# Decode attention with a gated MLP on one core: the last two heads' last keys loaded last over 128 partitions, six heads projected ahead of them, 24 heads projected in halves, result rows 4 apart

## The chip, the cores and the metric

One NeuronCore of a Trainium2 chip runs the kernel; the program uses 1 core. The metric is the device time of one execution in microseconds (us), median of the runs. TensorE (PE in the profile, its weight loads PEld), VectorE (DVE), ScalarE (ACT), GpSimd (POOL) and SyncE (SP) each work through a list of their own; DMAs are issued from the lists of SP and ACT.

## The reference: what is computed

One decode step for 8 sequences (B = 8, one new token each, D = 576), 32 heads of 128 elements, 4096 cached keys and values per head, all bf16:

```python
q = (x @ wq) -> [8, 32, 1, 128];  p = softmax(q . k_cache * 128**-0.5)
a = (p @ v_cache) -> [8, 1, 4096] @ wo
b = gelu(layernorm(x) @ w1 + b1) @ w2 + b2          # F = 4608
g = sigmoid((x * gate_w).sum(-1))
out = g * a + (1 - g) * b                            # [8, 1, 576]
```

The two caches hold 8 x 32 x 4096 x 128 x 2 bytes = 268 MB each, and every byte is read once.

## The kernel before

**Tiling.** The work goes through 32 groups n = 0 to 31; group n is 8 heads (head group hg = n // 8) of one sequence b = n % 8. A group's cache slice lies in SBUF as 128 partitions x 256 keys x 128 elements: partition = head x 16 + row, each row with 256 consecutive keys. That is 8192 KB for K and as much for V, with 64 KB in each partition. "Keys" below are these positions t = 0 to 255 of a partition.

**A group.** `scores` (line 488) takes 32 keys at a time: VectorE multiplies K by q (line 465), TensorE sums the products over slices of the 128 elements (lines 476 and 179), VectorE reduces the rest (line 484). `softmax` (line 500) makes E = exp(s - max) on ScalarE and P, which is E masked to each partition's own head, for all 8 heads (line 513). `pv` (line 520) multiplies P with V: four keys at a time, 32 columns of P as the weights and 4 x 128 elements of V as the moving side, in four column groups of the array. `evict` (line 538) copies the sum out of PSUM, `gather` (line 542) adds up the parts with a selection matrix, `total` (line 533) sums the softmax denominators, `norm` (line 549) divides, and `put` (line 455) writes the result into `OT_sb`, 128 elements x (32 heads x 8 sequences).

**Order.** The order on each engine is the order in which the Python code appends operations; `Stream.emit` puts semaphore waits before them. Groups 1 to 30 run in a loop on TensorE and VectorE. All K, V and weight loads are issued by SP, in order: K of group n + 1 when half of K of group n has been read (line 313), V of group n when `pv` of group n - 1 is done (line 324).

**The MLP** runs in group 0: `up_proj`, `act_h` (writes `hT_sb`), `down_proj` (line 601) with `quarters` (line 587), which splits the 576 output columns in four quarters of 144 (QN) and puts each on its own 32 partitions of PSUM bank `y_ps`, in rows 32 i to 32 i + 7. The last part of V of group 0 is issued after `down_proj`. `load_b2`, `b_gate` add the bias and multiply by 1 - g, into `bmg_sb`. `g4` holds g and 1 - g in the rows of `y_ps`.

**The end.** `to_rows` (line 626) rearranges heads 0 to 23 of `OT_sb` during the last group's scores, and `a_proj` (line 642) multiplies them with wo, 96 matmuls through `quarters`, into `y_ps`. V of the last group comes in 8 pieces of 128, 32, 32, 16, 16, 16, 8 and 8 keys (`V_LAST`, line 334). The first three go through `pv`, `evict` and `gather`; the last five (64 keys, `pv_turned`, line 649) with V as the weights and P's 8 columns as the moving side, so that they add to the gathered sum directly. Then follow `norm_turned` (line 660), `a_proj` of heads 24 to 31 (32 matmuls), one VectorE operation (line 735: g times the attention part plus `bmg_sb`), and 4 DMAs that write the result, two from SP and two from ACT.

Of the kernel before, what the change touches and what calls it, by code (L numbers as in the profile page):

```python
# [7 lines left out]
ALU = mybir.AluOpType  # L8
# [28 lines left out]
QP = 96 + B  # L37
# [103 lines left out]
def bass_gated_mix__mha_block_cached__mixer_channel_mlp__decode_kernel(  # L141
# [23 lines left out]
    def pstride(t):  # L165
        return t[tuple([slice(None)] * len(t.shape))].ap[0][0]
# [55 lines left out]
    hT_sb = sb("hT_sb", [128, NJ, B], BF16)  # L222
# [5 lines left out]
    OT_sb = sb("OT_sb", [128, H, B], BF16)  # L228
# [42 lines left out]
    def load(engine, dst, src, name, waits=()):  # L271
        return op(engine, lambda e: e.dma_start(dst, src), waits, dma=(nc.alloc_semaphore(name), 16))  # L272
# [9 lines left out]
    c_g4 = op("gpsimd", lambda e: e.memset(g4[:], 0.0))  # L282
    ld_x = load("scalar", x_sb, x_flat, "ld_x")
# [36 lines left out]
    def load_v(n, t0=0, t1=NTT, waits=()):  # L320
        nV[0] += 1
        src = kv_src(A_v_cache, n)[:, t0:t1, :]
        dst = VB[:, t0:t1, :]
        t = op("sync", lambda e: e.dma_start(dst, src), [*waits, v_done.get(n - 1)], dma=(sV, 16 * nV[0]))
        v_land[n] = [(t, VB, 0, 0, NTT)]

    def load_v_part(n, buf, at, t0, t1, waits):

        src = kv_src(A_v_cache, n)[:, t0:t1, :]
        dst = buf[:, at:at + t1 - t0, :]  # L330
        t = load("sync", dst, src, f"sVp{n}_{t0}", waits)
        v_land.setdefault(n, []).append((t, buf, at - t0, t0, t1))

    V_LAST = (128, 32, 32, 16, 16, 16, 8, 8)
    T_TURN = NTK + 64
# [119 lines left out]
    def put(n):  # L455
        hg, b = divmod(n, B)
        a_O[n] = op("scalar", lambda e: e.activation(  # L457
            out=OT_sb[:, hg * HB:(hg + 1) * HB, b], in_=O_n[:, :], func=ACT.Copy), [v_norm[n]])
# [61 lines left out]
    def pv(n, parts):  # L520
        for i in parts:
            land, buf, shift, t0, t1 = v_land[n][i]
            for tq in range(t0 // TQ, t1 // TQ):
                j, at = tq % 4, tq * TQ + shift
                o = o_ps[n // last][32 * j:32 * j + 32, :]
                w = [land, v_P[n], a_ev.get(n - 1), *c_ps] if tq == t0 // TQ else ()
                p_pv[n] = op("tensor", lambda e, o=o, tq=tq, at=at, buf=buf: e.matmul(  # L527
                    o, lhsT=(P if n < last else P_last)[:, tq, :, :].rearrange("p h t -> p (h t)"),
                    rhs=buf[:, at:at + TQ, :].rearrange("p t d -> p (t d)"),
                    start=(tq < 4), stop=(tq >= (NTQ if n < last else T_TURN // TQ) - 4)), w)  # L530
        v_done[n] = p_pv[n]
# [10 lines left out]
    def gather(n):  # L542
        o = oz_ps[:, 0:HB] if n < last else qb_ps[:, 0:HB]
        for tt in range(TQ):
            p_oz[n] = op("tensor", lambda e, tt=tt: e.matmul(  # L545
                o, lhsT=O_sb[:, tt, :], rhs=selO[:, tt, :], start=(tt == 0 and n < last), stop=(tt == TQ - 1 and n < last)),
                [a_ev[n], v_norm.get(n - 1), c_selO] if tt == 0 else ())
# [22 lines left out]
    def act_h():  # L570
        hb, t2 = (up[:, i, :] for i in range(2))
        b1b = bass.AP(tensor=b1_sb, offset=0, ap=[[pstride(b1_sb), 128], [1, NJ], [0, B]])
        t = op("scalar", lambda e: e.activation(out=hb, in_=up_ps[:, 0:NJ * B], func=ACT.Copy), [st["p_up"]])
        hbv = hb.rearrange("p (f b) -> p f b", b=B)
        t = op("gpsimd", lambda e: e.tensor_tensor(out=hbv, in0=hbv, in1=b1b, op=ALU.add), [t, ld_b1])
        t = op("gpsimd", lambda e: e.tensor_tensor(out=t2, in0=hb, in1=hb, op=ALU.mult), [t])
        t = op("gpsimd", lambda e: e.tensor_scalar(out=t2, in0=t2, scalar1=0.044715, scalar2=1.0, op0=ALU.mult,
                                                   op1=ALU.add), [t])
        t = op("gpsimd", lambda e: e.tensor_tensor(out=t2, in0=t2, in1=hb, op=ALU.mult), [t])
        t = op("scalar", lambda e: e.activation(out=t2, in_=t2, func=ACT.Sigmoid, scale=gelu_c), [t])  # L580
        st["v_h"] = op("gpsimd", lambda e: e.tensor_tensor(
            out=hT_sb[:].rearrange("p f b -> p (f b)"), in0=hb, in1=t2, op=ALU.mult), [t])
# [4 lines left out]
    def quarters(lhsT, w, first, stop, waits, end=aside):  # L587

        for i in range(4):
            last = (end if i == 3 else aside)("tensor", lambda e, i=i: e.matmul(  # L590
                y_ps[32 * i:32 * i + B, 0:QN], lhsT=lhsT, rhs=w[:, i * QN:(i + 1) * QN], start=first, stop=stop),
                waits if i == 0 else ())
        return last

    def load_b2():
        st["ld_b2"] = [
            load("scalar", b2_4[32 * i + r:32 * i + r + m, :],
                 bass.AP(tensor=B_b2.tensor, offset=B_b2.offset + i * QN, ap=[[0, m], [1, QN]]), f"ld_b2{i}_{r}", [c_b2])
            for i in range(4) for r, m in ((0, 5), (5, 3))]

    def down_proj(j0, j1):
        for jt in range(j0, j1):
            st["p_down"] = quarters(hT_sb[:, jt, :], w2_sb[:, jt, :], jt == 0, jt == NJ - 1,
                                    [st["ld_w2"], st["v_h"], c_yps] if jt == 0 else (),
                                    op if jt in (j0, NJ - 1) else aside)
            st.setdefault("p_down0", st["p_down"])
# [5 lines left out]
    def b_gate():  # L612
        t = op("gpsimd", lambda e: e.tensor_tensor(
            out=bmg_sb[0:QP, :], in0=bmg_sb[0:QP, :], in1=b2_4[0:QP, :], op=ALU.add), [st["a_bx"], *st["ld_b2"]])
        st["g_bmg"] = op("gpsimd", lambda e: e.tensor_scalar(
            out=bmg_sb[0:QP, :], in0=bmg_sb[0:QP, :], scalar1=g4[0:QP, 1:2], scalar2=None, op0=ALU.mult), [t, a_g4])

# [8 lines left out]
    def to_rows(hg):  # L626

        o = OT_sb[:, hg * HB:(hg + 1) * HB, :]
        a = bass.AP(tensor=OT_sb, offset=o.offset, ap=[[pstride(OT_sb), 128], [B, HB], [0, RD], [1, B]])
# [3 lines left out]
        for h in range(HB):  # L633
# [5 lines left out]
            out=o.rearrange("p r b -> p (r b)"), in_=up_ps[:, 0:RD * B], func=ACT.Copy), [st["p_rows"]])  # L639
        st["rows", hg] = st["a_rows"]  # L640

    def a_proj(hg):
        for h in range(hg * HB, (hg + 1) * HB):
            st["p_a"] = quarters(OT_sb[:, h, :], wo_sb[:, h, :], h == 0, h == H - 1,
                                 [st.get(("rows", hg)), a_O.get(min(hg * B + B - 1, NG - 2)), v_norm.get(NG - 1),
                                  st["ld_wo" if hg < NHG - 1 else "ld_wo3"], st["a_bx"]] if h == hg * HB else ())


    def pv_turned(n, parts):
        for i in parts:  # L650
            land, buf, shift, t0, t1 = v_land[n][i]
            for t in range(t0, t1):
                p_oz[n] = op("tensor", lambda e, t=t, buf=buf, at=t + shift: e.matmul(  # L653
                    qb_ps[:, 0:HB], lhsT=buf[:, at, :], rhs=P_last[:, t // TQ, :, t % TQ], start=(t == T_TURN), stop=(t == NTT - 1)),
                    [land, v_P[n]] if t == t0 else ())
# [4 lines left out]
    def norm_turned(n):  # L660
        hg, b = divmod(n, B)
        v_norm[n] = op("vector", lambda e: e.tensor_tensor(  # L662
            out=OT_sb[:, hg * HB:(hg + 1) * HB, b], in0=qb_ps[:, 0:HB], in1=rz[:, :], op=ALU.mult),
            [p_oz[n], v_rz[n]])
# [5 lines left out]
    for n in range(NG):  # L670
# [14 lines left out]
        if n == 0:  # L685
# [10 lines left out]
            for i in range(4):  # L696
                a_g4 = aside("scalar", lambda e, i=i: e.activation(out=g4[32 * i:32 * i + B, :], in_=stat[:, G_COL:G_COL + 2],
                                                                func=ACT.Copy), [v_omg, c_g4])
# [7 lines left out]
        if n == last:  # L706
            softmax(n)
            for hg in range(NHG - 1):
                a_proj(hg)
        pv(n - 1, (0,))  # L710
        evict(n - 1)
        gather(n - 1)
# [8 lines left out]
    t0 = 0  # L721
    for nt in V_LAST:
        load_v_part(last, VL, t0, t0, t0 + nt, [k_done[last, 0]])
        t0 += nt
    pv(last, (0,))
    total(last)
    recip(last)
    pv(last, (1, 2))
    evict(last)
    pv_turned(last, (3,))  # L730
    gather(last)
    pv_turned(last, range(4, len(V_LAST)))
    norm_turned(last)
    a_proj(NHG - 1)
    t = op("vector", lambda e: e.scalar_tensor_tensor(  # L735
        out=out_sb[0:QP, :], in0=y_ps[0:QP, 0:QN], scalar=g4[0:QP, 0:1], in1=bmg_sb[0:QP, :],
        op0=ALU.mult, op1=ALU.add), [st["p_a"], st["g_bmg"], a_g4])
    ld_out = [load(("sync", "scalar")[i % 2], out_flat[:, i * QN:(i + 1) * QN], out_sb[32 * i:32 * i + B, :],
                   f"ld_out{i}", [t]) for i in range(4)]
# [43 lines left out]
```

## Time and profile before

| | |
|---|---|
| median of 3 runs | 1298.19 us (1298.13 to 1298.19) |
| the profiled execution's own time | 1298.21 us |
| its span in the profile | 1296.3 us |
| busy: PE, PEld, DVE, ACT, POOL | 739.2, 152.9, 851.1, 68.8, 10.4 us |
| moved by DMA | 557.12 MB, 430 GB/s over the span |
| mean granted TensorE clock | 0.83 |

How to read it: the span runs from the first to the last recorded instruction; the execution's own time is 1.9 us longer. Start times below are microseconds from the start of the span. "L653" is line 653. A line of the chain of waits names a start, a length and what that stretch of the end-determining chain was spent on; a line of the timeline names start, length, engine, line, operation, output <- input and the count. In the windows view the columns are: window, its length, then busy time and number of instructions of PE, PEld, DVE, ACT and POOL, then the granted TensorE clock, the mean busy share of the 16 DMA engines, and GB/s.

### The profile page before, as it was taken

Reading aid. Unit: us, or ns where it says so; the run is one execution under the profiler, and the core shown is the slowest. Engines: PE = TensorE matmul, PEld = TensorE weight load, DVE = VectorE, ACT = ScalarE, POOL = GpSimd, SP = SyncE. Lnnn points to the kernel's source line nnn. Section 1 sums busy time; section 2 is a strip of 40 time slices with the busy share of each in tenths; the row PEclk is TensorE's granted clock in tenths of the full one; section 3 lists DMA queues with packets and bytes.
Section 4 is the critical chain, followed back from the end, with each engine's and each line's share of the span. In section 5 each row is a group of like instructions: output and inputs, shape, how many; then the busy total and the mean of one; then the engine's idle time right before and its main releaser. Section 6 shows DMA issues by size and latency. Waiting matters only on the chain.

```text
span 1296.3 us, 10765 instructions
## 1 busy us (share of the span) xinstructions
PE 739.2 (57%) x5044; PEld 152.9 (12%) x3252; DVE 851.1 (66%) x1075; ACT 68.8 (5%) x163; POOL 10.4 (1%) x23
## 2 busy tenths in 40 slices
PE   3955556555556555556555556645556655546646
PEld 0521111011111001111001111001111001111003
DVE  3646667766668766667766667766667776667771
ACT  3100000000000000000000000000000000000000
POOL 0010000000000000000000000000000000000000
PEclk8877898778888877888887799878789877888886
DMA  9999999999999999999999999999999999999997
GB/s 405 430 440 429 441 425 433 441 427 441 427 431 441 427 441 429 431 441 427 439 431 431 441 425 439 433 431 441 425 437 435 429 443 425 437 433 431 441 417 327
DMA packets 12987, 557.12 MB, mean 430 GB/s; under 512 B 1568, under 2 KB 2608, under 8 KB 3504
## 3 DMA queue, kind: packets, MB, share of 16 engines
q1 hardware_dynamic: 12704, 556.93, 99.5%
q8 instruction: 7, 0.11, 0.0%
q10 hardware_dynamic: 272, 0.04, 0.0%
q14 instruction: 4, 0.03, 0.0%
HBM read 556.96 MB, written 0.01 MB: 430 GB/s over the span
## 4 chain that ended last, share of the span: by engine, by line
DMA 68%; DVE 19%; PE 9%; issue 3%; SPq 0%; DVEq 0%
DMA KR<-in_A_k_cache_dram 67%; DVE p L465 16%; PE psb L179 7%; DVE s_sb L484 2%; DMA KR<-in_A_v_cache_dram 2%; PE psb L476 2%; SPq L272 0%; DVEq L134 0%; PE psb L590 0%; PE psb L653 0%; DVE out_sb L735 0%; DVE OT_sb L662 0%
## 5 line engine op out<-in xcount | busy, mean ns | idle before, releaser
L465 DVE TENSOR_TENSOR p<-KR,q_n 128x4096 bf16<-128x4096 bf16 x256 | 582.0, 2284 | 229.7 <-DMA KR<-in_A_k_cache_dram 229.7
L179 PE MATMUL psb<-p,ident 128*128 128x512 bf16 x1792 | 482.9, 415 | 0.0
L476 PE MATMUL psb<-p,ident 128*128 128x512 bf16 x256 | 111.4, 435 | 504.5 <-DVE p L465 504.5
L484 DVE TENSOR_REDUCE s_sb<-psb 128x32 f32<-128x512 f32 x256 | 175.2, 684 | 90.8 <-PE psb L179 90.8
L476 PEld LDWEIGHTS psb<-p,ident 128*128 128x128 bf16 x256 | 26.1, 102 | 950.9 <-DVE p L465 950.4
L527 PE MATMUL psb<-VB,P 128*32 128x512 bf16 x1984 | 115.0, 385 | 4.5 <-DMA VB<-in_A_v_cache_dram 4.5
L513 DVE TENSOR_SCALAR P<-E,own 128x256 bf16<-128x256 bf16 x248 | 51.7, 284 | 84.3 <-ACT E L510 84.3
L527 PEld LDWEIGHTS psb<-VB,P 128*32 128x32 bf16 x1984 | 50.6, 98 | 54.4 <-DMA VB<-in_A_v_cache_dram 4.7
L452 ACT ACTIVATE q_n<-q_bc 128x128 bf16<-128x128 bf16 x32 | 9.9, 309 | 865.9 <-DVE p L465 865.9
L545 PE MATMUL psb<-selO,O_sb 128*128 128x8 f32 x256 | 33.9, 259 | 21.8 <-ACT O_sb L539 21.8
L545 PEld LDWEIGHTS psb<-selO,O_sb 128*128 128x128 f32 x256 | 31.0, 191 | 37.1 <-ACT O_sb L539 37.1
L539 ACT ACTIVATE O_sb<-psb 128x512 f32<-128x512 f32 x32 | 19.1, 597 | 176.6 <-PE psb L527 176.6
L566 PE MATMUL psb<-yT_sb,KR 128*128 128x8 bf16 (+1 forms) x216 | 19.6, 229 | 0.0
L566 PEld LDWEIGHTS psb<-yT_sb,KR 128*128 128x128 bf16 (+1 forms) x216 | 18.4, 165 | 2.7 <-issue 1.4
L534 PEld LDWEIGHTS psb<-rs,ones 128*128 128x128 f32 x64 | 12.3, 194 | 46.0 <-issue 45.2
L510 ACT ACTIVATE E<-s_sb,mD 128x256 bf16<-128x256 f32 x32 | 16.0, 499 | 9.7 <-DVE mD L509 9.6
L501 DVE TENSOR_REDUCE mA<-s_sb 128x1 f32<-128x256 f32 x32 | 13.4, 420 | 1.1
L516 DVE TENSOR_REDUCE es<-E 128x1 f32<-128x256 bf16 x32 | 13.2, 412 | 0.0
L550 DVE RECIPROCAL rz<-psb 128x8 f32<-128x8 f32 x31 | 6.2, 201 | 9.0 <-PE psb L545 9.0
L457 ACT ACTIVATE OT_sb<-O_n 128x8 bf16<-128x8 bf16 x31 | 7.4, 237 | 84.5 <-DVE O_n L551 84.5
L534 PE MATMUL psb<-rs,ones 128*128 128x8 f32 x64 | 9.4, 219 | 0.0
L517 DVE TENSOR_SCALAR rs<-own,es 128x8 f32<-128x8 f32 x32 | 8.5, 265 | 1.1
(81 smaller groups left out, 109.7 us busy)
## 6 DMA issues: line engine op xcount, KB each, us to landing
KR<-in_A_k_cache_dram SPq DMA_DIRECT2D x2, 4096.0 KB, 27.2
VB<-in_A_v_cache_dram SPq DMA_DIRECT2D x1, 5376.0 KB, 21.0
VB<-in_B_w_dram SPq DMA_DIRECT2D x1, 5184.0 KB, 39.5
KR<-in_B_w_dram SPq DMA_DIRECT2D x1, 4608.0 KB, 43.3
VB<-in_A_wq_dram SPq DMA_DIRECT2D x1, 4096.0 KB, 12.6
KR<-in_A_v_cache_dram SPq DMA_DIRECT2D x1, 4096.0 KB, 17.9
KR<-in_A_wo_dram SPq DMA_DIRECT2D x1, 3456.0 KB, 24.7
VB<-in_A_v_cache_dram SPq DMA_DIRECT2D x1, 2816.0 KB, 38.7
```

The lines of the kernel that those rows point to most:

```text
L179: return e.add_instruction(mybir.InstMatmult(name=nc.get_next_instruction_name(), engine=mybir.EngineType.PE, ins=[e.lower_ap(rhs), e.lowe ...
L465: v_mult[n, c] = op("vector", lambda e: e.tensor_tensor(out=p1[:, par, :, :], in0=k, in1=qb, op=ALU.mult), [k_land[n, s], a_q[n], p_sum.ge ...
L476: fn = lambda e, r=r: e.matmul(tr_ps[par][:, :], lhsT=ident[:, :], rhs=r, start=True, stop=False)
L484: v_red[n, c] = op("vector", lambda e: e.tensor_reduce(out=s_sb[:, at:at + CT], in_=tr_ps[par][:, :].rearrange("p (t c) -> p t c", c=CH), ...
L501: t = op("vector", lambda e: e.tensor_reduce(out=mA[:, 0:1], in_=s_sb[:, :], axis=AX.X, op=ALU.max), [v_red[n, NC - 1], c_mA])
L510: a_exp[n] = op("scalar", lambda e: e.activation(out=E[:, :], in_=s_sb[:, :], func=ACT.Exp, bias=mD[:, 0:1], scale=1.0), [v_nm[n], v_P.get ...
L513: v_P[n] = op("vector", lambda e, h=h: e.tensor_scalar(out=(P if n < NG - 1 else P_last)[:, :, h, :], in0=E[:, :].rearrange("p (q t) -> p ...
L527: p_pv[n] = op("tensor", lambda e, o=o, tq=tq, at=at, buf=buf: e.matmul(o, lhsT=(P if n < last else P_last)[:, tq, :, :].rearrange("p h t ...
L534: p_z[n] = op("tensor", lambda e: e.matmul(oz_ps[:, HB:2 * HB], lhsT=ones[:, :], rhs=rs[:, :], start=True, stop=True), [v_rs[n], v_norm.ge ...
L539: a_ev[n] = op("scalar", lambda e: e.activation(out=O_sb[:].rearrange("p t d -> p (t d)"), in_=o_ps[n // last][:, :], func=ACT.Copy), [p_p ...
L545: p_oz[n] = op("tensor", lambda e, tt=tt: e.matmul(o, lhsT=O_sb[:, tt, :], rhs=selO[:, tt, :], start=(tt == 0 and n < last), stop=(tt == T ...
L566: st["p_up"] = (op if end else aside)("tensor", lambda e, w=w, o=o, kt=kt: e.matmul(o, lhsT=w, rhs=yT_sb[:, kt, :], start=(kt == 0), stop= ...
```

## The change

1. **V of the last group** comes in 10 pieces. Keys 0 to 159 of all heads: 64, 64, 32 (128 partitions, through `pv`). Keys 160 to 255 of the first six heads ("A": 96 partitions): 32, 32, 16, 16. Keys 160 to 255 of the last two heads ("B"): their 32 rows of 96 keys are laid out as 128 partitions x 24 keys, into the space of `q_bc`, in pieces of 8, 8, 8.
2. **Weights for B.** Their probabilities must lie on the same 128 partitions. `exp_wide` (ScalarE) makes exp again in f32 for them, `spread_P` (VectorE, 3 operations) normalizes them, and two small DMAs from SP copy them into `PW` (64 partitions x 24 elements each). `total` and `recip` move ahead of `pv` for this.
3. **The end.** After the A pieces `norm_turned` writes six heads and `norm_first` the partial sums of two; heads 24 to 27 are projected between the first B piece and the second; `norm_wide` finishes the last two heads; heads 28 and 29 are projected in the meantime, 30 and 31 last.
4. **24 heads in halves.** `a_proj_ahead` multiplies heads 0 to 23 with wo in 48 matmuls of 288 columns into bank `up_ps`, four ScalarE copies bring them to `A_f`, and GpSimd multiplies by g and adds them to `bmg_sb`.
5. **Result rows 4 apart.** `quarters` takes 32 weight columns with a stride through `hT_sb` or `OT_sb` (now sequence-major), so that sequence b lands on row 32 i + 4 b, with other sums on the rows between. `g4` is filled by 4 DMAs from ACT, `b2_4` by one DMA instead of 8, and the result is written by one DMA from SP instead of 4.
6. **`keep_busy`** puts 4, 1 and 3 matmuls of 512 columns, whose results nobody reads, between the pieces.

```diff
+    T_ALL = 160
+    HA = HB - 2
+    KW = (NTT - T_ALL) // 4
+    V_LAST = (("all", 64), ("all", 64), ("all", 32), ("A", 32), ("A", 32), ("A", 16), ("A", 16), ("B", 8), ("B", 8), ("B", 8))
+    def load_v_last(n, waits):
...
+            if kind == "B":
+                d = VW[:, t0:t1, :].rearrange("p t d -> p (t d)")
+                s = A_v_cache[b, hg * HB + HA]
+                s = bass.AP(tensor=s.tensor, offset=s.offset + (T_ALL + t0) * DH,
+                            ap=[[NTT * DH, 2 * RH], [KW * DH, 4], [1, nt * DH]])
+            else:
+                rows = 128 if kind == "all" else HA * RH
+                d, s = VL[0:rows, t0:t1, :], src[0:rows, t0:t1, :]
+            v_part.append((kind, t0, t1, load("sync", d, s, f"sVp{i}", waits)))
...
-    def quarters(lhsT, w, first, stop, waits, end=aside):
+    def quarters(t, n, j, w, first, stop, waits, end=aside):
+        lhsT = bass.AP(tensor=t, offset=j, ap=[[pstride(t), 128], [n // BS, 32]])
         for i in range(4):
             last = (end if i == 3 else aside)("tensor", lambda e, i=i: e.matmul(
-                y_ps[32 * i:32 * i + B, 0:QN], lhsT=lhsT, rhs=w[:, i * QN:(i + 1) * QN], start=first, stop=stop),
+                y_ps[32 * i:32 * i + 32, 0:QN], lhsT=lhsT, rhs=w[:, i * QN:(i + 1) * QN], start=first, stop=stop),
                 waits if i == 0 else ())
...
+    def a_proj_ahead():
+        h1 = H - HB
+        for h in range(h1):
+            lhsT = bass.AP(tensor=OT_sb, offset=h, ap=[[pstride(OT_sb), 128], [H // BS, 32]])
+            for i in range(2):
+                t = aside("tensor", lambda e, h=h, i=i, lhsT=lhsT: e.matmul(
+                    up_ps[64 * i:64 * i + 32, 0:2 * QN], lhsT=lhsT, rhs=wo_sb[:, h, 2 * i * QN:2 * (i + 1) * QN],
+                    start=(h == 0), stop=(h == h1 - 1)), [st["rows", NHG - 2], st["ld_wo"]] if h == i == 0 else ())
...
+    def spread_P(n):
+        h = HA * RH
+        t = op("vector", lambda e: e.tensor_tensor(out=rs[h:, :], in0=own[h:, :], in1=rz[h:, :], op=ALU.mult), [v_rz[n]])
+        t = op("vector", lambda e: e.tensor_reduce(out=rz_p[h:, :], in_=rs[h:, :], axis=AX.X, op=ALU.add), [t])
+        t = op("vector", lambda e: e.tensor_scalar(
+            out=P_n[h:, :, 0:KW], in0=E_f[h:, :, 0:KW], scalar1=rz_p[h:, 0:1], scalar2=None, op0=ALU.mult), [t, st["a_Ef"]])
...
+            s = bass.AP(tensor=p1, offset=(h + RH * i) * p + P_n.offset, ap=[[p, RH], [32, 4], [1, KW]])
+            d = bass.AP(tensor=PW, offset=64 * i * q + 32 * i, ap=[[q, 64], [1, KW]])
+            st["ld_PW"].append(load("sync", d, s, f"ld_PW{i}", [t, c_PW]))
...
+    def keep_busy(n):
+        for i in range(n):
+            r = wo_sb[:, i, 0:512]
+            if i == 0:
+                fn = lambda e, r=r: e.matmul(tr_ps[1][:, :], lhsT=ident[:, :], rhs=r, start=True, stop=(n == 1))
+            else:
+                fn = lambda e, r=r, i=i: held(e, tr_ps[1][:, :], ident[:, :], r, i == n - 1)
+            aside("tensor", fn, [v_red[last, NC - 1], st["ld_wo"]] if i == 0 else ())
...
+            p_oz[n] = op("tensor", lambda e, o=o, v=v, p=p, t=t, stop=(end and t == t1 - 1): e.matmul(
+                o, lhsT=v, rhs=p, start=(kind == "B" and t == 0), stop=stop),
+                [land, w, *(st["ld_PW"] if w is None else ())] if t == t0 else ())
...
-    pv(last, (0,))
+    load_v_last(last, [k_done[last, 0], a_q[last]])
     total(last)
     recip(last)
-    pv(last, (1, 2))
+    spread_P(last)
+    pv(last, v_part[0][3], *v_part[0][1:3])
+    keep_busy(4)
+    pv(last, v_part[1][3], *v_part[1][1:3])
+    keep_busy(1)
+    pv(last, v_part[2][3], *v_part[2][1:3])
     evict(last)
-    pv_turned(last, (3,))
-    gather(last)
-    pv_turned(last, range(4, len(V_LAST)))
-    norm_turned(last)
-    a_proj(NHG - 1)
+    keep_busy(3)
+    gather(last, qb_ps[:, 0:HB], False)
+    for i in range(3, 7):
+        pv_turned(last, i)
+    v_A = norm_turned(last)
+    norm_first(last)
+    pv_turned(last, 7)
+    a_proj(H - HB, H - HB + 4, [v_A])
+    pv_turned(last, 8)
+    pv_turned(last, 9)
+    v_B = norm_wide(last)
+    a_proj(H - HB + 4, H - 2, [v_A])
+    a_proj(H - 2, H, [v_B])
...
-    ld_out = [load(("sync", "scalar")[i % 2], out_flat[:, i * QN:(i + 1) * QN], out_sb[32 * i:32 * i + B, :],
-                   f"ld_out{i}", [t]) for i in range(4)]
+    ld_out = [load("sync", by_quarters(out_flat, D), batch_rows(out_sb, QN), "ld_out", [t])]
```

More of the change, by code (lines that the diff above doesn't have):

```diff
@@ L221, in bass_gated_mix__mha_block_cached__mixer_channel_mlp__decode_kernel @@
     b2_4 = sb("b2_4", [128, QN], BF16)
-    hT_sb = sb("hT_sb", [128, NJ, B], BF16)
+    hT_sb = sb("hT_sb", [128, B * NJ + NJ], BF16)
+    hT_b = view(hT_sb, 0, [128, B, NJ])
     Q4 = sb("Q4", [128, 4 * NJ * B], BF16)
@@ L227, in bass_gated_mix__mha_block_cached__mixer_channel_mlp__decode_kernel @@
     q_bc = sb("q_bc", [128, B, NHG * DH], BF16)
-    OT_sb = sb("OT_sb", [128, H, B], BF16)
+    OT_sb = sb("OT_sb", [128, B * H + H], BF16)
+    OT_b = view(OT_sb, 0, [128, B, H])
+    VW = view(q_bc, 0, [128, (B * NHG), DH])
+    PW = sb("PW", [128, 2, 32], BF16)
+    X2 = sb("X2", [128, 2], F32)
+    E_f = view(p1.bitcast(F32), CT * DH // 2 + 2 * QN, [128, 4, 32])
+    P_n = view(p1, CT * DH + 6 * QN, [128, 4, 32])
+    rz_p = sb("rz_p", [128, 1], F32)
+    A_f = view(p1.bitcast(F32), CT * DH // 2, [128, QN])
     bmg_sb = view(up_f, 0, [128, QN])
@@ L457, in put @@
         a_O[n] = op("scalar", lambda e: e.activation(
-            out=OT_sb[:, hg * HB:(hg + 1) * HB, b], in_=O_n[:, :], func=ACT.Copy), [v_norm[n]])
+            out=OT_b[:, b, hg * HB:(hg + 1) * HB], in_=O_n[:, :], func=ACT.Copy), [v_norm[n], c_OT])
     def mult(n, c):
@@ L518, in softmax, with pv @@
             out=rs[:, :], in0=own[:, :], scalar1=es[:, 0:1], scalar2=None, op0=ALU.mult), [t, p_z.get(n - 1)])
[L520 to L530, printed above, removed]
+    def pv(n, land, t0, t1):
+        for tq in range(t0 // TQ, t1 // TQ):
+            j, at = tq % 4, tq * TQ
+            o, v = o_ps[n // last][32 * j:32 * j + 32, :], VB if n < last else VL
+            w = [land, v_P[n], a_ev.get(n - 1), *c_ps] if tq == t0 // TQ else ()
+            p_pv[n] = op("tensor", lambda e, o=o, tq=tq, at=at, v=v: e.matmul(
+                o, lhsT=(P if n < last else P_last)[:, tq, :, :].rearrange("p h t -> p (h t)"),
+                rhs=v[:, at:at + TQ, :].rearrange("p t d -> p (t d)"),
+                start=(tq < 4), stop=(tq >= (NTT if n < last else T_ALL) // TQ - 4)), w)
         v_done[n] = p_pv[n]
@@ L540, in evict, with gather @@
                                                       func=ACT.Copy), [p_pv[n], p_oz.get(n - 1)])
-    def gather(n):
-        o = oz_ps[:, 0:HB] if n < last else qb_ps[:, 0:HB]
+    def gather(n, o, stop=True):
         for tt in range(TQ):
             p_oz[n] = op("tensor", lambda e, tt=tt: e.matmul(
-                o, lhsT=O_sb[:, tt, :], rhs=selO[:, tt, :], start=(tt == 0 and n < last), stop=(tt == TQ - 1 and n < last)),
+                o, lhsT=O_sb[:, tt, :], rhs=selO[:, tt, :], start=(tt == 0), stop=(tt == TQ - 1 and stop)),
                 [a_ev[n], v_norm.get(n - 1), c_selO] if tt == 0 else ())
@@ L638, in to_rows @@
         st["a_rows"] = aside("scalar", lambda e: e.activation(
-            out=o.rearrange("p r b -> p (r b)"), in_=up_ps[:, 0:RD * B], func=ACT.Copy), [st["p_rows"]])
+            out=o.rearrange("p b r -> p r b"), in_=up_ps[:, 0:RD * B].rearrange("p (r b) -> p r b", b=B),
+            func=ACT.Copy), [st["p_rows"]])
         st["rows", hg] = st["a_rows"]
[L642 to L646, printed above, removed]
@@ L649, in pv_turned @@
[L649 to L655, printed above, removed]
+    def a_proj_ahead():
[6 more added lines that the diff above has]
+                    start=(h == 0), stop=(h == h1 - 1)), [st["rows", NHG - 2], st["ld_wo"]] if h == i == 0 else ())
+        for i in range(4):
+            t = aside("scalar", lambda e, i=i: e.activation(
+                out=A_f[32 * i:32 * i + 32, :], in_=up_ps[64 * (i // 2):64 * (i // 2) + 32, i % 2 * QN:(i % 2 + 1) * QN],
+                func=ACT.Copy), [t] if i == 0 else ())
+        t = op("gpsimd", lambda e: e.tensor_scalar(
+            out=A_f[0:QP, :], in0=A_f[0:QP, :], scalar1=g4[0:QP, 0:1], scalar2=None, op0=ALU.mult), [t, *st["a_g4"]])
+        st["g_bmg"] = op("gpsimd", lambda e: e.tensor_tensor(
+            out=bmg_sb[0:QP, :], in0=bmg_sb[0:QP, :], in1=A_f[0:QP, :], op=ALU.add), [t, st["g_bmg"]])
@@ new lines, in a_proj, with exp_wide @@
+    def a_proj(h0, h1, normed):
+        for h in range(h0, h1):
+            st["p_a"] = quarters(OT_sb, H, h, wo_sb[:, h, :], h == H - HB, h == H - 1,
+                                 [a_O[NG - 2], *normed, st["ld_wo3"], st["a_bx"]] if h == h0 else ())
+    def exp_wide(n):
+        h = HA * RH
+        st["a_Ef"] = op("scalar", lambda e: e.activation(
+            out=E_f[h:, :, 0:KW], in_=s_sb[h:, T_ALL:].rearrange("p (s k) -> p s k", s=4), func=ACT.Exp,
+            bias=mD[h:, 0:1], scale=1.0), [v_nm[n]])
@@ L695, in bass_gated_mix__mha_block_cached__mixer_channel_mlp__decode_kernel @@
                                                            scalar1=-1.0, scalar2=1.0, op0=ALU.mult, op1=ALU.add), [a_g])
-            for i in range(4):
-                a_g4 = aside("scalar", lambda e, i=i: e.activation(out=g4[32 * i:32 * i + B, :], in_=stat[:, G_COL:G_COL + 2],
-                                                                func=ACT.Copy), [v_omg, c_g4])
+            st["a_g4"] = a_g4 = [load("scalar", batch_rows(g4, 2, i), stat[:, G_COL:G_COL + 2], f"ld_g4{i}", [v_omg, c_g4])
+                    for i in range(4)]
             down_proj(0, NJ)
@@ L707, in bass_gated_mix__mha_block_cached__mixer_channel_mlp__decode_kernel @@
             softmax(n)
-            for hg in range(NHG - 1):
-                a_proj(hg)
-        pv(n - 1, (0,))
+            exp_wide(n)
+            a_proj_ahead()
+        pv(n - 1, v_land[n - 1], 0, NTT)
         evict(n - 1)
-        gather(n - 1)
+        gather(n - 1, oz_ps[:, 0:HB])
         if n < last:
```

72 lines of the change are left out of this document (46 added, 26 removed).

## The prediction, made before the changed kernel ran

> **What bounds the kernel now.** First the page: the DMA queues, the rates by slice, and the chain that ended last.
>
> ```profile
> GB/s 405 430 440 429 441 425 433 441 427 441 427 431 441 427 441 429 431 441 427 439 431 431 441 425 439 433 431 441 425 437 435 429 443 425 437 433 431 441 417 327
> ...
> q1 hardware_dynamic: 12704, 556.93, 99.5%
> ...
> DMA 68%; DVE 19%; PE 9%; issue 3%; SPq 0%; DVEq 0%
> ```
>
> SP's queue keeps the 16 DMA engines busy for 99.5% of the span, and no slice between the first and the last stands out. The bytes are the same after the change, so nothing can be won or lost ahead of the last slice unless the queue runs dry. What is left is the end; the chain of waits, in order of time, shows it:
>
> ```profile
> 1267.23 24.38 DMA KR<-in_A_v_cache_dram
> 1291.61 0.05 issue
> 1291.66 0.39 PE psb L653 x8
> 1292.05 0.02 issue
> 1292.07 0.20 DVE OT_sb L662
> 1292.28 0.04 issue
> 1292.32 1.16 PE psb L590 x32
> 1293.48 0.03 issue
> 1293.51 0.37 DVE out_sb L735
> ```
>
> The last 8 keys of V land at 1291.61. Their 8 matmuls, the norm and 32 projections take 1.90 us to the final VectorE operation at 1293.51; the output fills the rest to 1296.3. So the whole stake is 4.7 us (0.36%), and a change that only shortens this end can't reach 0.2% (2.6 us, about what a measurement of this kernel can tell from no change). The timeline of TensorE and its neighbours there:
>
> ```profile
> 1243.47 2.84 PE L179 MATMUL psb<-p,ident 128*128 128x512 bf16 x7
> ...
> 1263.75 3.91 SPq L272 DMA_DIRECT2D KR<-in_A_v_cache_dram  x8
> ...
> 1264.00 1.67 PE L179 MATMUL psb<-p,ident 128*128 128x512 bf16 x7
> ...
> 1265.73 1.67 PE L590 MATMUL psb<-KR,OT_sb 128*8 128x144 bf16 x96
> ...
> 1271.92 5.89 PE L527 MATMUL psb<-VB,P 128*32 128x512 bf16 x64 [4.52 <-DMA VB<-in_A_v_cache_dram]
> ...
> 1278.53 1.06 PE L545 MATMUL psb<-selO,O_sb 128*128 128x8 f32 x8 [0.71 <-ACT O_sb L539]
> ...
> 1279.86 0.17 DVE L551 TENSOR_TENSOR O_n<-psb,rz 128x8 bf16<-128x8 f32 x1
> ...
> 1281.64 3.60 PE L527 MATMUL psb<-KR,p 128*32 128x512 bf16 x32 [2.06 <-DMA KR<-in_A_v_cache_dram]
> ...
> 1285.18 0.60 PE L534 MATMUL psb<-rs,ones 128*128 128x8 f32 x2
> ...
> 1285.81 0.21 DVE L658 RECIPROCAL rz<-psb 128x8 f32<-128x8 f32 x1 [5.78 <-PE psb L534]
> ...
> 1287.35 0.60 ACT L539 ACTIVATE O_sb<-psb 128x512 f32<-128x512 f32 x1 [7.05 <-PE psb L527]
> ...
> 1287.88 0.56 PE L653 MATMUL psb<-p,KR 128*128 128x8 bf16 x16 [0.59 <-DMA KR<-in_A_v_cache_dram]
> ...
> 1290.40 0.99 PE L653 MATMUL psb<-p,KR 128*128 128x8 bf16 x24 [0.67 <-DMA KR<-in_A_v_cache_dram]
> ```
>
> Each of these waits tells a landing: keys to 127 at 1281.6, to 207 at 1287.9, to 239 at 1290.4, to 255 at 1291.6. That is 78 ns per key (80 keys in 6.24 us, 32 in 2.52, 16 in 1.21), 32 KB each. The windows view gives the clock:
>
> ```profile
> 1283.60:1287.00 3.40, 3.40 (x34) 1.09 (x26) 0.21 (x1) 0.00 (x0) 0.00 (x0) 0.53 1.00 402
> 1287.00:1290.40 3.40, 2.14 (x48) 1.76 (x41) 0.00 (x0) 0.60 (x1) 0.00 (x0) 0.97 0.81 318
> 1290.40:1293.80 3.40, 2.47 (x64) 1.90 (x64) 0.49 (x2) 0.00 (x0) 0.00 (x0) 0.50 0.02 7
> ```
>
> TensorE runs its last stretch at half clock: 32 projections in 1.16 us there, 96 in 1.67 earlier.
>
> **Part by part: what is hidden.** `down_proj` loads 32 weight columns for each of its 144 matmuls instead of 8, and the last part of V of group 0 is issued behind it:
>
> ```profile
> 14.70 5.59 PE L428 MATMUL psb<-VB,p 128*8 128x512 bf16 x40 [3.04 <-DMA VB<-in_A_wq_dram]
> ...
> 47.56 30.69 SPq L324 DMA_DIRECT2D VB<-in_A_v_cache_dram  x2
> ...
> 73.40 4.49 PE L590 MATMUL psb<-VB,hT_sb 128*8 128x144 bf16 x144 [4.83 <-POOL hT_sb L581]
> ```
> ```profile
> VB<-in_A_v_cache_dram SPq DMA_DIRECT2D x1, 2816.0 KB, 38.7
> ...
> KR<-in_B_w_dram SPq DMA_DIRECT2D x1, 4608.0 KB, 43.3
> ...
> KR<-in_B_w_dram SPq DMA_DIRECT2D x1, 576.0 KB, 44.2
> ```
>
> The load ahead of it, issued at 47.6, lands 38.7 us later, at 86.3, while `down_proj` ends at 77.9: 8 us of cover by the landing. The matmuls could double (4.5 us) unseen; without cover, each microsecond would count in full. The four `g4` DMAs stand in ACT's list where four copies stood, `load_b2` becomes one issue instead of eight, three memsets join GpSimd's start, where TensorE waits for wq until 14.7 anyway: nothing. `a_proj_ahead` has 48 matmuls of 288 columns for 96 of 144, the same columns but in two column groups instead of four: 1.67 us becomes 3.3, in the 4.52 us that TensorE waits for V of group 30. Its four copies and two GpSimd operations have 20 us until they are needed. Were that cover gone, `pv` of group 30 would start later, and it has slack of its own: the first piece of V of group 31 now lands 64 keys earlier, but nothing behind it ends before the last landing.
>
> **The stream.** SP issues 10 pieces, 8 took 3.91 us, so about 4.9 from 1263.75; the queue holds V of group 30 until 1271.9, so they follow without a gap; their second wait, for the last copy out of `q_bc`, ends in group 30. Two more pieces: 0.05 us, between nothing and 0.2 (16 KB rows became 2 KB rows at no more than 1 ns per key above). The A pieces are the unknown: every large load in the trace spans 128 partitions, these 96. By bytes an A key takes 0.75 x 78 = 58 ns, 5.6 us for 96; by length of row it takes 78, 7.5 us. I take bytes, since 96 rows are six for each of 16 engines as 128 are eight, and the row nearest to it is the 78 ns that did not change with the length of the rows. Landings by that: key 159 at 1284.1, A at 1286.0, 1287.9, 1288.8, 1289.8, B at 1290.4, 1291.0, 1291.66.
>
> **TensorE before B.** `total` goes ahead to 1280.1 (after the norm, 1279.86 + 0.17), 0.60; `pv` of 64 keys 1.8 (half of 3.60); four `keep_busy` at 0.24 to 0.41 (1.67 / 7 and 2.84 / 7), 1.3; 64 keys 1.6; one more 0.3; 32 keys 0.85: 1286.5. Eviction 0.7, with three `keep_busy` beside it, and 1.06 of `gather`: 1288.3. Then 96 keys at 35 ns (0.56 / 16; 41 by 0.99 / 24): 3.4 to 3.9, to 1291.7 or 1292.2. That is right where B becomes ready.
>
> **The added wait.** The first B matmul waits for both PW copies, and behind it on TensorE stand the 16 projections of heads 24 to 27, the other 16 B matmuls and the last 16 projections; VectorE's `norm_wide`, the final operation and SP's output wait for those. `recip` now ends near 1281.0, three VectorE operations near 0.2 follow, and SP issues the copies about 1281.8, long after the V pieces on its queue. That queue serves in order: the 576 KB load, 1.4 us by itself, lands 44.2 us after its issue, behind the 4608 KB load. So the copies move only after the last piece of V. Their price isn't in the trace: nothing at least, one 8-key piece (0.62) at most, which has as many rows; they carry 6 KB, not 256, so I take 0.2. The first B matmul starts at 1291.66 + 0.2 + 0.05 = 1291.91.
>
> **The sum from there.** 24 B matmuls 0.84 to 0.99 (0.56 x 24 / 16; the x24 row), 0.90; 16 projections 0.28 to 0.57 (at 1.67 / 96 and 1.13 / 32; the chain's 1.16 includes its tail), 0.40; `norm_wide` as the norm of before, 0.26 with its gaps, heads 28 and 29 beside it; 8 projections 0.14 to 0.39, 0.30, and a 0.03 gap: final operation at 1293.80, against 1293.51: **+0.29**. I take middles because the fuller TensorE may hold its clock. The output:
>
> ```profile
> L272 SPq DMA_DIRECT2D out_dram<-out_sb x2: 298/333/368, 1293.9 to 1294.3; - x2
> ```
>
> SP's second output issue starts about 0.4 after its first; with one issue the data starts that much earlier, less if 32 rows take longer to issue than 8: **-0.30**, between 0 and -0.4. Sum: 0.29 - 0.30, about nothing. On the profiled execution's own 1298.21 (span 1296.3 and 1.9 around it; the median is 1298.19) that gives **1298.2 us**; with its terms at their ends 1297.5 to 1299.0.
>
> **Rivals.**
>
> *Six rows per engine isn't what an A piece costs* (the other side). The mechanism is the slowest engine or memory side of the 96 partitions: if it carries r rows of 24 KB instead of six, A takes r / 6 x 5.6 us, and all landings behind it shift. With r = 8 (an A key as slow as any other, 78 ns) that is +1.9: 1300.1, still no measurable difference. From r = 9 on (more than 2.6 us) it decides for slower; at r = 12, half the engines' or half the memory's rate, +5.6: 1303.8. For it: the trace has no large load under 128 partitions, so it shows 430 GB/s for one layout only, and DMA is what ends last. Against: rows of 8 KB down to 2 KB ran at the same 76 to 79 ns per key, which looks like engines that each work through equal rows. Chances: 0.20 for about eight, 0.20 for nine or more.
>
> [...]
>
> *The PW copies overtake V* (the change gains): B then waits for V alone, two of its pieces and heads 24 to 27 are done ahead, and after 1291.66 stand 0.05 + 0.39 + 0.26 + 0.30 + 0.03: final operation at 1292.69, -0.82, with the output -1.1: 1297.1. For it: they are issued ten microseconds early. Against: the 44.2 us of the 576 KB load. 0.08.
>
> *TensorE becomes the bound* before B: at half clock throughout, with `keep_busy` (8 x 0.41) in the way instead of beside the eviction, A ends near 1292.9 rather than 1291.7, and the B matmuls wait a further 1.0: 1299.2. For it: the clock stayed at 0.53 while TensorE was busy all of 1283.6 to 1287.0. Against: it then rose to 0.97, and the new stream is fuller. 0.10.
>
> **How the numbers follow.** Forecast 0.42, eight rows 0.20, nine or more 0.20, TensorE 0.10, overtaking 0.08. The range leaves out the nine rows or more: 1296.9 (overtaking, with its ends) to 1300.9 (eight rows with the forecast's upper end); the likeliest case alone 1297.5 to 1299.0. Slower by over 0.2% (above 1300.8): nine rows and a little of the eight, 0.22. Faster (below 1295.6): only if most of the end vanished, 0.01. Within 0.2%: 0.77.
>
> **What would show it.** In the profile after, the last V landing at 1291.7 (six rows) or 1293.5 and later; the idle time before the first A matmuls and what ended it; the wait of TensorE ahead of the first B matmul, released by a DMA into PW just after the last V piece (in order) or by V at 1290.4 (overtaking), or no wait at all (TensorE bound); the granted clock from 1287 on; 1.89 us from the first B matmul to the final operation; one output issue. The prediction is wrong if the DMA queue runs dry in group 0, if the A pieces land late by more than 2 us, or if the copies take longer than a V piece.

## The result, and the profile after

The changed kernel takes **1305.09 us** (median of 6 runs, 1304.28 to 1305.69), the kernel before in the same runs 1298.12: a ratio of 1.0053, 95% interval 1.0042 to 1.0064. It is 7.0 us slower. The prediction, 1298.2 with a range to 1300.9, was wrong; the time lies 1.3 us above its rival of twelve rows (1303.8), to which, with all from nine rows on, it gave 0.20. The profiled execution took 1304.28 us, its span is 1302.5.

One thing ahead of the rest: the text and the diff ahead of the prediction have the two PW copies on SP (`load("sync", ...)`). That is wrong. The changed kernel says `load("scalar", ...)`, so ACT issues them, and the prediction's "added wait" rests on the wrong queue.

The page of the profile after, the lines that stood first before:

```profile
GB/s 403 446 422 435 435 427 441 429 439 429 441 427 443 423 441 429 435 435 427 439 431 439 429 441 427 439 427 441 429 435 435 427 439 431 439 429 439 427 417 251
...
q1 hardware_dynamic: 12868, 556.94, 99.5%
...
DMA 69%; DVE 19%; PE 9%; issue 3%; SPq 0%; DVEq 0%
```

The last slice but one moves 417 GB/s in both; only the last falls, from 327 to 251. TensorE takes up V of group 30 at 1271.62, where it was 1271.92 before. So nothing was lost in group 0 or in the loop. The chain of waits at the end:

```profile
1267.53 29.40 DMA KR<-in_A_v_cache_dram
1296.93 0.05 issue
1296.97 0.61 PE psb L738 x16
1297.58 0.02 issue
1297.60 0.17 DVE OT_sb L747
1297.78 0.04 issue
1297.82 0.71 PE psb L617 x16
1298.53 0.52 PE psb L738 x16
1299.05 0.75 PE psb L617 x13
1299.80 0.03 issue
1299.82 0.37 DVE out_sb L836
```

The chain hangs on the last A piece (keys 240 to 255 of six heads), which lands at 1296.93; the forecast was 1289.8. The B pieces, issued after it, land 29.2 us after their issue, the last at 1298.5, just ahead of its matmuls, so they don't end the chain. TensorE's timeline shows which landings were late:

```profile
1271.62 3.64 PE L554 MATMUL psb<-VB,P 128*32 128x512 bf16 x64 [1.97 <-DMA VB<-in_A_v_cache_dram]
...
1281.41 1.05 PE L554 MATMUL psb<-KR,p 128*32 128x512 bf16 x16 [1.55 <-DMA KR<-in_A_v_cache_dram]
...
1287.05 1.04 PE L554 MATMUL psb<-KR,p 128*32 128x512 bf16 x8 [4.27 <-DMA KR<-in_A_v_cache_dram]
...
1293.66 1.01 PE L738 MATMUL psb<-p,KR 96*128 96x8 bf16 x32 [1.82 <-DMA KR<-in_A_v_cache_dram]
1295.33 0.59 PE L738 MATMUL psb<-p,KR 96*128 96x8 bf16 x16 [0.65 <-DMA KR<-in_A_v_cache_dram]
1296.97 0.59 PE L738 MATMUL psb<-p,KR 96*128 96x8 bf16 x16 [1.05 <-DMA KR<-in_A_v_cache_dram]
1297.42 0.35 PE L738 MATMUL psb<-PW,q_bc 128*128 128x2 bf16 x8
```

Key 127 is on time (1281.4), key 159 comes at 1287.05 instead of 1284.1, and A stays late. TensorE waits each time, so it isn't the bound; for the first B matmul it waits for nothing. The windows view, first of the kernel before, then of the changed one (the last three columns are the granted clock, the DMA engines' busy share and GB/s):

```profile
1284.00:1288.00 4.00, 3.41 (x35) 1.06 (x28) 0.21 (x1) 0.60 (x1) 0.00 (x0) 0.65 1.02 407
```
```profile
1284.00:1288.00 4.00, 0.95 (x8) 0.14 (x8) 0.00 (x0) 0.00 (x0) 0.00 (x0) 0.52 1.00 191
1288.00:1292.00 4.00, 3.84 (x47) 2.91 (x41) 0.00 (x0) 0.60 (x1) 0.00 (x0) 0.50 0.99 228
1292.00:1296.00 4.00, 1.61 (x48) 1.44 (x48) 0.00 (x0) 0.00 (x0) 0.00 (x0) 0.50 0.96 246
```

This is the line to learn to see: the busy share stays at 1.0 and the rate halves. The engines aren't short of work; each packet takes twice as long: in the trace's packet records the median packet of 8 KB that starts in the first of these windows took 314 ns before and 599 ns after. Here the DMA engines' busy share was no measure of what they moved: 1.00 at 191 GB/s, 1.02 at 407 before.

### The profile page after: what moved, and what is told of

It is laid out like the page before. It is cut to its first block, busy times and chain, and to the rows that moved or that the text cites. A ratio compares the mean times of both kernels' runs of the same rounds, so it can differ in the third digit from the quotient of the medians.

```text
span 1302.5 us, 10785 instructions
## 1 busy us (share of the span) xinstructions
PE 741.1 (57%) x5052; PEld 155.7 (12%) x3255; DVE 852.4 (65%) x1080; ACT 69.4 (5%) x164; POOL 16.1 (1%) x28
## 3 DMA queue, kind: packets, MB, share of 16 engines
q1 hardware_dynamic: 12868, 556.94, 99.5%
## 4 chain that ended last, share of the span: by engine, by line
DMA 69%; DVE 19%; PE 9%; issue 3%; SPq 0%; DVEq 0%
DMA KR<-in_A_k_cache_dram 66%; DVE p L494 16%; PE psb L180 7%; DVE s_sb L513 2%; DMA KR<-in_A_v_cache_dram 2%; PE psb L505 1%; SPq L283 0%; DVEq L135 0%; PE psb L617 0%; PE psb L738 0%; DVE out_sb L836 0%; DVE OT_sb L747 0%
```

## The experiments

The theory after this profile: loads that touch 96 partitions run at about half rate because of where those partitions lie. Rivals: it is the B layout, the copies or the new end; it is the split of 96 rows over 16 engines; each partition has a rate of its own; it is the side that is read, since with the partitions the rows of the cache change too.

**Same kernel, A over all 128 partitions.**

```diff
-                rows = 128 if kind == "all" else HA * RH
+                rows = 128
```

> The changed kernel with its A pieces loaded over all 128 partitions (786 KB more to move, 1.8 us at 430 GB/s; the extra rows are not used). If the shape of the A pieces, 96 partitions, is what made V late, moving more is faster: last V near 1293.5, time near 1300.2. If it is the B pieces, the two PW copies or the new end, this stays near 1305 or goes to 1307.

Measured: 1299.24 us (1298.89 to 1300.69), ratio to before 1.001 (1.0 to 1.002). Moving 786 KB more is 5.9 us faster than the changed kernel, and 1.0 better than expected. Windows and chain of this run:

```profile
1284.00:1288.00 4.00, 3.22 (x51) 2.03 (x49) 0.00 (x0) 0.60 (x1) 0.00 (x0) 1.00 1.02 412
```
```profile
1267.81 24.10 DMA KR<-in_A_v_cache_dram
...
1294.92 0.37 DVE out_sb L836
```

At the same busy share the rate is back at 412. So the shape of the A loads is the cause, not B, the copies or the end: those are all still in it.

**The kernel before, with nothing but the shape of its last loads changed.**

```diff
...
-        t = load("sync", dst, src, f"sVp{n}_{t0}", waits)
+        if t0 < 160:
+            t = [load("sync", dst, src, f"sVp{n}_{t0}", waits)]
+        else:
+            t = [load("sync", dst[a:b, :, :], src[a:b, :, :], f"sVp{n}_{t0}_{a}", waits) for a, b in ((0, 96), (96, 128))]
...
```

> The kernel before, nothing of the change but the shape of the last loads: each piece from key 160 on is loaded as partitions 0 to 95 and then 96 to 127, same bytes, same order of work. If the 96-partition loads alone carry the loss: by the loads measured alone 72 keys took 8.2 us on 96 partitions and 3.1 on 32, so 96 keys take up to 15.1 us instead of 7.5, and from half of that on if the two overlap: 1302 to 1306. If the loss needs the rest of the change: 1298.3.

Measured: 1304.36 us (2 runs), ratio 1.0049 (1.0031 to 1.0067). The windows view of this run:

```profile
1284.00:1288.00 4.00, 1.46 (x22) 0.44 (x14) 0.21 (x1) 0.00 (x0) 0.00 (x0) 0.92 0.92 197
1288.00:1292.00 4.00, 0.82 (x8) 0.16 (x8) 0.00 (x0) 0.00 (x0) 0.00 (x0) 0.50 1.02 248
```

So the shape is enough by itself: the old kernel shows the same half rate, and nothing else of the change is in it. (The other 32 partitions are a load of their own here, so this run has 96 and 32 partitions and six loads more.)

**Each A piece in two loads, 0 to 31 and 32 to 95.**

```diff
...
+                if kind == "A":
+                    more = load("sync", VL[0:32, t0:t1, :], src[0:32, t0:t1, :], f"sVq{i}", waits)
+                    d, s = VL[32:96, t0:t1, :], src[32:96, t0:t1, :]
...
```

> The changed kernel, each A piece in two loads: partitions 0 to 31, then 32 to 95; the same bytes on the same partitions. Halves theory (partitions 0 to 63 share one half of the memory's DMA side, 64 to 127 the other, 215 GB/s each): 32 to 95 touches both halves evenly and runs at 430 GB/s, 0 to 31 at 215, together 7.3 us for A where 96 rows cost about 12: time near 1300.2. Uneven-split theory (96 rows do not divide well over 16 engines, 64 and 32 do): 5.6 us, time near 1298.5. Per-partition theory (a partition takes 3.4 GB/s, so the rate goes by the number of partitions): 7.5 + 7.5 us, time near 1308.

Measured: 1302.58 us, ratio 1.0035 (1.0022 to 1.0048): 2.5 us better than 96 in one load, on the same partitions, but 2.4 us above the halves theory's number, 4.1 above the uneven split's and 5.4 below the per-partition theory's. No theory is hit. The halves theory is nearest; its two halves were the author's conjecture, with 215 GB/s as half of the 430 of the whole span, and the next two runs test its principle.

**The loads alone.** One load at a time, no computing; the output is zeros. Each shape is loaded with 24 and with 96 keys, four times in one run.

```diff
...
+    SHAPES = (("from0_128", 0, 128), ("from0_96", 0, 96), ("from16_96", 16, 112), ("from0_64", 0, 64),
+              ("from32_64", 32, 96), ("from0_32", 0, 32), ("from48_32", 48, 80))
...
```

> Loads alone, one at a time, of 24 and of 96 keys (6 and 24 KB rows), no computing and an output of zeros; the difference of the two landings is the time for 72 keys, free of what each load costs anyway. Halves theory: 128 partitions 5.5 us; 64 from partition 0 5.5, 64 from partition 32 2.7; 32 from 0 2.7; 96 from 0 at least 5.5 and up to 8.2 if engines block each other; 96 from 16 at least 4.1 and up to 8.2. Uneven-split theory: 64 partitions 2.7 wherever they start, 32 1.4, both 96 alike above 4.1. Per-partition theory: 5.5 for all seven.

The windows view of the 96-key loads, first to seventh shape in the order above (window, its length, GpSimd, clock, DMA share, GB/s):

```profile
6.00:14.40 8.40, 0.00 (x0) 1.00 0.95 374
20.00:31.20 11.20, 0.00 (x0) 1.00 0.93 211
37.00:47.80 10.80, 0.00 (x0) 1.00 0.89 207
54.30:62.30 8.00, 0.00 (x0) 1.00 0.88 187
68.00:72.60 4.60, 0.00 (x0) 1.00 0.81 315
76.70:80.60 3.90, 0.00 (x0) 1.00 0.80 170
85.10:89.00 3.90, 0.00 (x0) 1.00 0.78 176
```

Row four against row five: 64 partitions, the same bytes, as many rows of the same length, and 187 or 315 GB/s (with most of a load's start and end in it) according to whether they begin at 0 or at 32. That excludes the uneven split and a rate per partition. But 96 from 16, with 48 rows in either half, is as slow as 96 from 0, and 32 from 48 as slow as 32 from 0. Two halves are too coarse.

**More shapes.**

```diff
+    SHAPES = (("a", 0, 112), ("b", 0, 80), ("c", 0, 48), ("d", 64, 128), ("f", 16, 80), ("g", 32, 128), ("h", 32, 96))
```

> Loads alone as before (24 and 96 keys, one at a time), more shapes, in this order: 0 to 111, 0 to 79, 0 to 47, 64 to 127, 16 to 79, 32 to 127, 32 to 95. What is open is why 96 partitions from 16, with 48 rows in each half, were as slow as 96 from 0. [...] If only the two halves counted: 16 to 79 4.1, 32 to 127 5.4, 0 to 47 4.1.

The DMA view, issue to landing; 96 keys first, then 24 keys for the same letters:

```profile
a<-in_A_k_cache_dram SPq DMA_DIRECT2D x4, 2688.0 KB, 12.5
g<-in_A_k_cache_dram SPq DMA_DIRECT2D x4, 2304.0 KB, 12.5
...
f<-in_A_k_cache_dram SPq DMA_DIRECT2D x4, 1536.0 KB, 9.6
h<-in_A_k_cache_dram SPq DMA_DIRECT2D x4, 1536.0 KB, 6.2
c<-in_A_k_cache_dram SPq DMA_DIRECT2D x4, 1152.0 KB, 10.8
a<-in_A_k_cache_dram SPq DMA_DIRECT2D x4, 672.0 KB, 4.2
g<-in_A_k_cache_dram SPq DMA_DIRECT2D x4, 576.0 KB, 3.9
...
f<-in_A_k_cache_dram SPq DMA_DIRECT2D x4, 384.0 KB, 3.9
h<-in_A_k_cache_dram SPq DMA_DIRECT2D x4, 384.0 KB, 3.2
c<-in_A_k_cache_dram SPq DMA_DIRECT2D x4, 288.0 KB, 3.5
```

The difference is the time of 72 keys: 32 to 95 (h) 3.0 us; 16 to 79 (f), as many rows, 5.7, where two halves say 4.1; 0 to 47 (c) 7.3 for fewer rows than h, where they say 4.1 as well; 32 to 127 (g) 8.6, where they say 5.4; 0 to 111 (a) 8.3. Of all shapes tried only 32 to 95 (1.18 MB in 3.0 us, 393 GB/s) and the full 128 (374 GB/s with a load's start and end in it) come near the 430 GB/s of the whole span. The other two shapes took 6.1 (64 to 127) and 7.2 (0 to 79). So two halves fail in f, c and g, by 1.4 to 1.8 times. What sets the rate of each shape, and which rows go to which engine, isn't shown here and stays open.

**The copies behind V, on SP's queue** (with A over 128 partitions).

```diff
-            st["ld_PW"].append(load("scalar", d, s, f"ld_PW{i}", [t, c_PW]))
+            st["ld_PW"].append(load("sync", d, s, f"ld_PW{i}", [t, c_PW]))
```

> The version with A over 128 partitions, and the two PW copies issued by SP behind V instead of by ACT. If SP's queue serves in order, the first B matmul waits for the copies, which land after the last piece of V: the final operation about 1 us later than in that version (1299.24), 1300.2. If copies overtake, no difference: 1299.2.

Measured: 1301.06 us, ratio 1.0024 (1.0014 to 1.0033), 1.8 us above the same kernel with ACT's queue (about 1 was expected). Its timeline:

```profile
1294.18 0.35 PE L738 MATMUL psb<-PW,q_bc 128*128 128x2 bf16 x8 [1.68 <-DMA PW<-p]
```

The copies, issued from 1280.9 on behind V on SP's queue, land at 1294.05, 12.4 us after the first of them was issued (on ACT's queue, in the same kernel, they took 6.0 to 6.6 us), and TensorE waits 1.68 us for 6 KB. The prediction's step was right about that queue and applied to the wrong one.

**Parts 4 and 5 alone**, with V's pieces and the end's order of the kernel before:

```diff
-    T_ALL = 160
-    HA = HB - 2
+    T_ALL = 192
+    HA = HB
...
-    V_LAST = (("all", 64), ("all", 64), ("all", 32), ("A", 32), ("A", 32), ("A", 16), ("A", 16), ("B", 8), ("B", 8), ("B", 8))
+    V_LAST = (("all", 128), ("all", 32), ("all", 32), ("A", 16), ("A", 16), ("A", 16), ("A", 8), ("A", 8))
...
```

> Only parts 4 and 5 of the change (24 heads in halves, rows 4 apart, one output load), with V's pieces and the end's order as before. If the loss is all V's: 1298.0, between 1297.7 and 1298.5 (the output was 0.1 us shorter in the changed kernel, the last 32 projections load four times the weight columns). If these parts carry some of the loss, above 1299.

Measured: 1298.03 us, ratio 0.9999 (0.9989 to 1.0009). They neither gain nor cost anything that this measurement can tell.

**All of the idea, every load over 128 partitions.** Keys 160 to 255 of all four head pairs in B's layout, 24 keys per partition; the weights come straight from E:

```diff
-                rows = 128 if kind == "all" else HA * RH
-                d, s = VL[0:rows, t0:t1, :], src[0:rows, t0:t1, :]
+            if kind != "all":
+                j = 3 if kind == "B" else kind
+                d = (VW[:, t0:t1, :] if j == 3 else VL[:, T_ALL + KW * j:T_ALL + KW * (j + 1), :]).rearrange("p t d -> p (t d)")
+                s = A_v_cache[b, hg * HB + 2 * j]
...
+            s = bass.AP(tensor=E, offset=32 * j * p + T_ALL, ap=[[p, 32], [KW, 4], [1, KW]])
```

> The changed kernel with every load over 128 partitions: keys 160 to 255 of all four head pairs are laid out as B is, 24 keys in each partition, and the weights for it are copied from E right after the exponentials (4 copies from ACT) and masked by VectorE. Same bytes as before. If the shape of the loads was the whole loss, V ends as before (last landing 1291.7) and the shorter end shows: final operation near 1293.0 instead of 1293.5, time 1297.6, from 1297.2 to 1298.0. If the wide layout or the copies cost V something of their own, above 1298.2.

And the same without part 6:

```diff
-    keep_busy(4)
...
-    keep_busy(1)
...
-    keep_busy(3)
```

> The same without the eight matmuls whose results nobody reads. If they keep TensorE's clock up where it counts, the end after the last landing runs at half clock and takes 0.3 to 0.6 us longer: 1298.0. If not: 1297.6, as with them.

Measured: 1297.74 us with the idle matmuls, ratio 0.9998 (0.9989 to 1.0007), and 1297.78 without, 0.9997 (0.9988 to 1.0006). The 7 us are gone, which closes the case on the shape of the loads. It closes the rival of the reading side too: in the loads alone, the rows read moved together with the partitions written, but here each pair of heads reads 32 rows of 96 keys, as the loads on 32 partitions did, and writes 128 partitions. The timeline with the idle matmuls shows the first matmuls of two such pieces, each released by its landing, 1.85 us apart:

```profile
1288.13 0.78 PE L741 MATMUL psb<-p,KR 128*128 128x2 bf16 x24 [0.26 <-DMA KR<-in_A_v_cache_dram]
1289.98 0.80 PE L741 MATMUL psb<-p,KR 128*128 128x2 bf16 x24 [1.07 <-DMA KR<-in_A_v_cache_dram]
```

That is 786 KB at 425 GB/s, where loads on 32 partitions got 170 and 176.

The end is shorter, but by its own size only: the final operation starts at 1293.03 in the profile, 1293.51 before. The idle matmuls do nothing for the time. With them the granted clock is 0.87 from 1287.0 to 1290.4 and 0.50 from there on; in the next version, without them and with another order of the end, it is 0.50 in both stretches. But with and without them in this order, both chains of waits hang on a landing at 1289.9, and the projections behind it take 0.71 and 0.79 us in both. One more order of the end, with heads 24 to 29 projected earlier:

```diff
+    a_proj(H - HB, H - HB + 4, [v_A])
+    pv_turned(last, 5)
+    pv_turned(last, 6)
+    v_B = norm_wide(last, 2)
     pv_turned(last, 7)
...
+    a_proj(H - HB + 4, H - 2, [v_B])
...
```

> All loads over 128 partitions, no idle matmuls, and a new order at the end, since TensorE worked without a gap from 1290.0 to 1293.0 in the version before it: heads 24 to 27 are normed after the second pair and projected while the third is awaited, the third pair comes in 16 and 8 keys, heads 28 and 29 are projected between the first and second B piece, only 30 and 31 after the last. Last landing 1291.65, then 8 matmuls 0.39, norm 0.26, 8 projections 0.35: final operation at 1292.65 instead of 1293.03, time 1297.3. If TensorE is behind anyway: 1297.7 as in the version before it.

Measured: 1297.58 us, ratio 0.9996 (0.9987 to 1.0005). The final operation stayed where it was (1293.07, where 1292.65 was expected); the windows view of this run says why:

```profile
1287.00:1290.40 3.40, 3.14 (x78) 2.85 (x79) 0.60 (x4) 0.00 (x0) 0.00 (x0) 0.50 0.91 346
1290.40:1293.80 3.40, 2.32 (x61) 1.68 (x58) 0.69 (x3) 0.00 (x0) 0.00 (x0) 0.50 0.07 26
```

TensorE is busy 3.14 of 3.40 us at half clock, and behind: this run's chain of waits goes through its work, and the eviction and norms between, from 1285.0 on, without a DMA. All three wide versions measure 0.3 to 0.4 us below the before of their runs, and no interval excludes no change.

## Why the prediction was wrong, point by point

- **The step that failed: "I take bytes" for the A pieces.** The term was 5.6 us for 96 keys; loads of that shape alone run at 207 to 211 GB/s, 11.3 us (2.36 MB at 209 GB/s), which is the rival's r = 12. That rows are shared out evenly over the 16 engines, six or eight for each, was the author's assumption; no run shows it, nor an engine or a side of the memory that carries twelve. In the kernel the last A piece lands 7.1 us later than forecast (1296.93, not 1289.8). The forecast let B start 2.1 us after that landing and it starts 0.5 after, so the first B matmul is 5.5 us late (1297.42, not 1291.91); the stretch from there is 0.5 longer and the output 0.2 longer than forecast. That is the 6.2 us by which the span grew in the profiled execution. The median lies a further 0.8 above that execution, which stays open. The reason given, that rows of 8 KB to 2 KB had run at the same 78 ns, varied the length of a row and held the partitions at 128; it couldn't speak for another number of partitions. The text said itself that no large load under 128 partitions was in the trace, and still gave the cases that go by bytes 0.60.
- **Why 7.1 and not 5.7.** The 128-partition piece ahead of A is late too, by 2.9 us at key 159; A itself takes 9.9 us from there, 4.2 more than forecast. Packets of A begin while the earlier piece is still under way, as the packet records show: the earlier piece has 128 packets of 8 KB, and 231 of that size had begun by 1287.0, when it landed; packets of 8 KB took 309 to 325 ns up to 1281.1 and over 500 ns from 1281.5 to 1287.0. That they slow each other fits the run that split A in two and also came out 2.4 us over its number, but it is argued, not shown.
- **The added wait.** There is none, since the copies go through ACT's own queue. The source line and view of the changed kernel:

```profile
L283 ACTq DMA_DIRECT2D PW<-p x2: 607/630/653, 1278.9 to 1279.6; - x2
...
DMA to landing us min/median/max: 9.7/10.6/11.5
```

  They land by 1291.1, ahead of need at 1297.4 (and ahead of the forecast's 1291.9). On that ground alone the forecast should have been lower, by the 0.2 us that it took for the copies at least.
- **What is hidden was right.** `down_proj` took 4.55 us instead of 4.49 and `a_proj_ahead` 3.16 against 3.3 forecast; parts 4 and 5 alone change nothing that could be measured. The DMA queue never ran dry (99.5% before and after).
- **TensorE before B** was earlier than forecast: `pv` of group 30 ran its 64 matmuls in 3.64 us instead of 5.89 and `total` began at 1277.5, not 1280.1, so that rival fell here. With A over 128 partitions TensorE still waits for loads ahead of B (0.64 us for the last A piece there), so it isn't the bound in that run either. Only in the last order of the end is it behind ahead of B.
- **The sum from B**, 1.89 us, was 2.40 (1297.42 to 1299.82) and 2.36 with A over 128 partitions. The 24 B matmuls fit (0.90 against 0.87 to 0.96); 16 projections took 0.64 to 0.71 instead of 0.40, with the granted clock at 0.50 from 1296 on, where the forecast took a middle; and the last 16 took 0.75 where 0.56 stood for norm and projections.
- **The output**, -0.30, gained 0.1: the single issue takes 0.68 us where one of the four took 0.33. The line of the timeline:

```profile
1300.21 0.68 SPq L283 DMA_DIRECT2D out_dram<-out_sb  x1
```

## What to carry to other kernels

Loads alone ran at 374 GB/s on 128 partitions and at 207 to 211 on 96, so repacking all the bytes over 128 partitions (1297.74 us), or even moving 786 KB more (1299.24), was faster here than loading fewer rows (1305.09); with 64 rows, 32 to 95 ran at 315 GB/s and 0 to 63 at 187. In the profile look at GB/s beside the DMA share: a share of 1.00 at 191 GB/s meant here that each packet of 8 KB took longer (a median of 599 ns, not 314), not that the queue was without work. And where every row of a trace shares one layout, an edit that changes that layout has no row, and its price belongs in the forecast at its bad end until one load alone has been measured.

## What the runs showed of the hardware

- 48 partitions (0 to 47) took 7.3 us for 72 keys, longer than 64 at 32 to 95 (3.0) and than 64 at 16 to 79 (5.7). Fewer rows took longer here.
- 32 weight columns with a stride instead of 8 neighbours cost nothing that shows over the 144 matmuls of `down_proj`: 4.55 us against 4.49.
- One output DMA of 32 rows is issued in 0.68 us, one of 8 rows in 0.30 to 0.37.
- With matmuls whose results nobody reads, the granted clock from 1287.0 to 1290.4 was 0.87; in the last version, which has none, it was 0.50. With the same order of the end, the time was as it was without them (1297.74 against 1297.78).
